# The last layer (768 to 512) as seven products over halves instead of plain blocks

## Chip, cores and metric

The kernel runs on one core of a Trainium2 chip. The metric is the time of one execution on the device in microseconds (us); before the change the median of three runs is 1456.44 us (1456.42 to 1460.39).

## What is computed

A linear attention with a norm, then an MLP with softplus, then an MLP with the maximum of three products; 4608 tokens, all in fp32.

```python
kv = einsum('bhsd,bhse->bhde', k, v)                    # 64 x 64 per head
x = q @ kv;  x = x / sqrt(mean(x*x) + 1e-06) * g_norm   # 4608 x 512
g = softplus(x @ w_in)                                  # 512 -> 2048
x = g @ w_out                                           # 2048 -> 512
h = maximum(maximum(x @ w1, x @ w2), x @ w3)            # 512 -> 768
out = h @ moe2_w_out                                    # 768 -> 512: the last layer
```

## The kernel before

The tokens are cut into five passes of 2 x 464 (the last 2 x 448). Features lie on the 128 partitions, the tokens of one half (t = 0 or 1) in a tile's columns. A pass has four stages: H (16 row blocks of w_in, softplus), X (w_out), layer 2 (w1, w2, w3 and their maximum) and the last layer. The attention of the next pass runs beside layer 2.

H, X and layer 2 multiply 2 x 2 blocks (rows by halves, inputs by halves, tokens by halves) in seven products instead of eight: `product` forms product m = 1 to 7 of a group g of two row blocks into the PSUM banks X, Y and W (`BANK`), and `sums` (L350) adds them up. Products 1, 6, 7 and 4 go into one X bank one after another; between them ACT copies the bank out, and VectorE adds Y or W to the copy. Group starts are 7 steps apart while a group spans 13 (`SLOT`), so the products of two groups alternate on TensorE. The inputs of the seven products are made by `combine` (L289): differences on VectorE and GpSimd, then each is split into hi and lo halves (an fp32r cast on ACT and a subtraction, `split`, L120). In passes 1 to 4 a product block is three fp32r matmuls (`mm3`, L130 to 134: hi x hi, hi x lo, lo x hi); in pass 0 it is one fp32 matmul on weights converted there (`to_f32`).

The weights of passes 1 to 4 come as split units of up to two product numbers from DRAM (`load_unit`, L183) into a ring of four tiles `u` (two `u3` for half units, one `ux` for a group's first). Weights that are converted late in pass 0 (`LATE`, and the last layer's) are kept there unsplit; pass 1 loads them as fp32 (`load_sums`, tile `st`, two buffers), splits them on ACT and VectorE into `u` (`split_unit`) and stores the unit for passes 2 to 4 (`make_later`, L210).

The last layer alone has plain blocks (`out_part`, L696): output block e = 0 to 3 and token half t, sums over six row blocks f in two parts (4 and 2). One loaded unit serves both t. Its input is the split maximum (`hl`, `hh`, L668 on), the lo half on GpSimd. In passes 1 to 3 the next pass's first two H groups are stretched and start `SHARED` = 12 steps early, so that they alternate with the parts of the last layer.

All work is put in as events with a time in steps (`at`); one step is about six matmuls. The framework then orders each engine's instructions by priorities and its own estimates; an engine works in that order.

Of the kernel before, what the change touches and what calls it, by code (L numbers as in the profile page):

```python
# [1 line left out]

# [14 lines left out]
P = 128  # L17
# [22 lines left out]
SHARED = 12  # L40
# [5 lines left out]
def kernel(  # L46
# [54 lines left out]
    def ge_tile(p, name, n):  # L101
        return gc_tile(name, n) if p == 0 else wide(pools["ge"], "ge", GE_BUFS, name, n)
# [62 lines left out]
    G_2 = [[16 + 3 * f + j for j in range(3)] for f in range(NF2 // 2)]  # L165
    UNITS = ((1, 5), (6, 2), (7, 4), (3,))
# [84 lines left out]

    def convert(g, i):
        if i == 0:
            sw[g] = pools["raw"].tile([P, 7, 256], F32, tag="sw", bufs=3, name="sw")
        w = sw[g]
        if i == 0:
            dst = w[:, PLACE[1]:PLACE[2] + 1:PLACE[2] - PLACE[1]]
        else:
            dst = w[:, PLACE[5]:PLACE[4] + 1:PLACE[4] - PLACE[5]]
        to_f32(raws.pop((g, i)), dst)  # L260

    def sums_of_weights(g):
        w = sw[g]
        a11, s1, s2, a12, s3, a22, s4 = (w[:, PLACE[m]] for m in (1, 5, 6, 2, 7, 4, 3))
# [14 lines left out]
    def convert_out(j, i):  # L279

        if i == 0:
            sw["o", j] = pools["raw"].tile([P, 3, 512], F32, tag="sw", bufs=3, name="swo")
        to_f32(raws.pop(("o", j, i)), sw["o", j][:, i])

# [4 lines left out]
    def combine(tile, dst, c, tiles, steps, t2_bank, on_dve=()):  # L289
# [4 lines left out]
        for s in steps:  # L294
            for m in STEPS[s]:
                hi, lo = tile("hi", n, F32R), tile("lo", n, F32R)
                src = {1: b11, 2: b21, 3: b22, 7: b12, 4: b11}.get(m)
# [3 lines left out]
                elif m == 6:  # L301
                    src = t2 = psum(t2_bank, "t2")[:, 0:n]
# [37 lines left out]
    def run_group(base, p, g, rhs, after, stretch=1):  # L340
# [6 lines left out]
        for m in ORDER:  # L347
            at(base + stretch * SLOT[m], step, m)
# [219 lines left out]
    def run_pass(pas, base):  # L568
# [5 lines left out]
        def weights_at(t, g, stretch=1):  # L574
# [35 lines left out]
        for fp in range(8):  # L610
            t = start[f"H{fp}"]
            weights_at(t, G_H[fp], stretch.get(f"H{fp}", 1))
            run_group(t, pas, G_H[fp], R,
                      sums(lambda w, src, fp=fp: h_done(fp, w, src), lambda w: (ctile(f"h{w}", N), w != 11),
                           nc.vector if pas and fp == 0 else nc.scalar),
                      stretch.get(f"H{fp}", 1))
        for n in range(4):
            gc[n] = {}
            if n == 0 or pas == 0:
                for c in range(2):  # L620
                    at(start[f"H{2 * n + c}"] + 12 * stretch.get(f"H{2 * n + c}", 1) + 0.5, combine_g, n, ALL, (c,))
# [34 lines left out]
        hh = {}  # L656
        mx = {}

        def h2_done(fp, j, w, src):
# [9 lines left out]
            if j == 2:  # L669
                src = mx.pop(key)  # L670
                at_ = 2 * fp + w // 20, w % 10 - 1
                if pas == 0:
                    hh[at_] = src
                else:
                    hi, lo = gc_tile("hh", N, F32R), gc_tile("hl", N, F32R)
                    split(nc.scalar, src, hi, lo, nc.gpsimd)
                    hh[at_] = (hi, lo)

        for k in range(9):
            fp, j = divmod(k, 3)  # L680
            t = base2 + 7 * k
            weights_at(t, G_2[fp][j])
            run_group(t, pas, G_2[fp][j], R2,
                      sums(lambda w, src, fp=fp, j=j: h2_done(fp, j, w, src),
                           lambda w, j=j: ((ge_tile(pas, f"m{w}", N), True) if j == 0
                                          else (ctile(f"m{w}", N), w == 22))))
# [179 lines left out]
```

## Time and profile before

| | before |
|---|---|
| median of 3 runs | 1456.44 us (1456.42 to 1460.39) |
| profiled execution | 1454.81 us, span 1453.0 us, mean granted clock 0.996 |
| TensorE (PE) busy | 1412.1 us, 97% |
| VectorE (DVE) / ScalarE (ACT) / GpSimd (POOL) busy | 52% / 50% / 46% |
| DMA | 315.5 MB, 217 GB/s on average |

The profile shows one execution. Its own time is larger than its span by 1.8 us, which lie around the span. "PE" is TensorE's matmuls, "PEld" its weight loads, which overlap; a matmul's duration overlaps with the next one's, so spacing is read from starts. "ACT", "DVE" and "POOL" are ScalarE, VectorE and GpSimd; "SP" issues the DMAs. In tile names u, u3, ux are weight units, st fp32 weights to be split, Xh, Xx, Xo (Y, W) the banks of H, X and layer 2, oacc the last layer's, Xy, Yy, Wy those of the last layer after the change, m the maxima, og the attention's output.

### The profile page before, as it was taken

How to read it: one execution, taken by the hardware profiler on the slowest of the kernel's cores; microseconds unless marked ns; L12 is line 12 of the kernel's file. 1: busy time of each engine (PE TensorE's matmuls, PEld its weight loads, DVE VectorE, ACT ScalarE, POOL GpSimd, SP SyncE). 2: the span in 40 equal slices, each digit the busy share in tenths (PEclk: the TensorE clock that was granted, in tenths of full speed). 3: DMA queues.
4: the chain of work that ended last, by engine and by line, in shares of the span. 5: the costliest groups of instructions: out<-in, count | busy, mean ns of one | idle time of the engine just before them, and what ended most of it. 6: DMA issues, size and time to landing. Idle time of an engine off the chain costs nothing.

```text
span 1453.0 us, 18314 instructions
## 1 busy us (share of the span) xinstructions
PE 1412.1 (97%) x6164; PEld 1126.8 (78%) x6164; DVE 761.4 (52%) x1204; ACT 719.6 (50%) x1370; POOL 671.7 (46%) x613
## 2 busy tenths in 40 slices
PE   6899999999999999999999999999999999999998
PEld 4344445554688888788888898888889888998998
DVE  4654565677144566763445557144574544447341
ACT  5566545565164437754543466254436634543321
POOL 3697778444044453452534335343463453435211
PEclk9999999999999999999999999999999999999999
DMA  7677778854366776866667776566666656676672
GB/s 279 225 253 250 272 250 315 303 176 138 129 211 210 217 242 222 266 239 200 203 209 220 247 257 193 171 209 211 217 214 207 201 181 206 211 219 208 195 219 93
DMA packets 107948, 315.51 MB, mean 217 GB/s; under 512 B 12112, under 2 KB 23632, under 8 KB 107856
## 3 DMA queue, kind: packets, MB, share of 16 engines
q1 hardware_dynamic: 107856, 314.36, 66.5%
q8 instruction: 49, 0.80, 0.3%
q14 instruction: 43, 0.35, 0.1%
HBM read 248.78 MB, written 65.54 MB: 216 GB/s over the span
## 4 chain that ended last, share of the span: by engine, by line
PE 83%; DMA 5%; DVE 4%; ACT 3%; issue 2%; POOL 2%; SPq 0%; ACTq 0%; POOLq 0%; DVEq 0%
PE Xh L132 4%; PE Xx L134 4%; PE Xx L132 4%; PE Xx L133 4%; PE Xh L134 4%; PE Xh L133 4%; PE Xo L133 3%; PE Xo L132 3%; PE Xo L134 3%; PE Xo L330 3%; PE Xh L330 3%; PE oacc L704 3%; PE oacc L133 3%; PE oacc L134 2%; PE oacc L132 2%
## 5 line engine op out<-in xcount | busy, mean ns | idle before, releaser
L122 POOL TENSOR_TENSOR lo<-e,hi 128x464 fp32r<-128x464 f32 (+1 forms) x160 | 187.4, 1202 | 216.8 <-ACT hi L116 213.3
L128 POOL TENSOR_TENSOR e<-e 128x464 f32<-128x464 f32 (+1 forms) x40 | 50.6, 1264 | 157.2 <-DVE t L128 157.2
L116 ACT COPY m<-Xo 128x464 f32<-128x464 f32 (+1 forms) x135 | 72.3, 541 | 81.3 <-PE Xo L134 71.3
L116 ACT CAST hi<-t 128x464 fp32r<-128x464 f32 (+1 forms) x96 | 52.3, 545 | 121.3 <-DVE e L128 56.3
L125 DVE TENSOR_TENSOR x<-x,Xx 128x464 f32<-128x464 f32 (+1 forms) x120 | 75.6, 632 | 61.9 <-PE Xx L134 55.2
L122 POOL TENSOR_TENSOR hl<-m,hh 128x464 fp32r<-128x464 f32 (+1 forms) x48 | 58.8, 1227 | 97.0 <-ACT hh L116 96.9
L122 POOL TENSOR_TENSOR u<-sw,u 128x512 fp32r<-128x512 f32 (+1 forms) x76 | 87.9, 1184 | 19.2 <-ACT u L116 19.0
L116 ACT CAST hi<-e 128x464 fp32r<-128x464 f32 (+1 forms) x160 | 85.7, 578 | 21.9 <-PE Yx L133 18.7
L526 POOL TENSOR_TENSOR og<-og,r 128x464 f32<-128x464 f32 (+1 forms) x32 | 41.2, 1289 | 107.5 <-DVE r L516 103.1
L152 ACT ACTIVATE e<-h 128x464 f32<-128x464 f32 (+1 forms) x80 | 47.3, 591 | 82.5 <-DVE h L125 81.9
L132 PE MATMUL Xo<-hi,u 128*128 128x464 f32 (+1 forms) x228 | 86.6, 380 | 1.2 <-ACT m L116 1.2
L134 PE MATMUL Xo<-hi,u 128*128 128x464 f32 (+1 forms) x228 | 84.8, 372 | 0.0
L133 PE MATMUL Xo<-lo,u 128*128 128x464 f32 (+1 forms) x228 | 84.8, 372 | 0.0
L116 ACT COPY h<-Xh 128x464 f32<-128x464 f32 (+1 forms) x108 | 58.7, 544 | 47.6 <-PE Xh L134 33.0
L128 POOL TENSOR_TENSOR sw<-sw 128x256 f32<-128x256 f32 x75 | 56.7, 756 | 48.5 <-DVE sw L243 34.8
L125 DVE TENSOR_TENSOR h<-h,Yh 128x464 f32<-128x464 f32 (+1 forms) x80 | 50.6, 633 | 52.7 <-ACT h L116 25.0
L125 DVE TENSOR_TENSOR Wh<-h,Wh 128x464 f32<-128x464 f32 (+1 forms) x40 | 25.7, 642 | 93.5 <-PE Wh L134 67.1
L132 PE MATMUL Xh<-hi,u 128*128 128x464 f32 (+1 forms) x194 | 72.3, 373 | 0.0
L122 DVE TENSOR_TENSOR lo<-t,hi 128x464 fp32r<-128x464 f32 (+1 forms) x96 | 60.4, 633 | 22.0 <-ACT hi L116 20.8
L134 PE MATMUL Xh<-hi,u 128*128 128x464 f32 (+1 forms) x194 | 71.8, 370 | 0.0
L133 PE MATMUL Xh<-lo,u 128*128 128x464 f32 (+1 forms) x194 | 71.8, 370 | 0.0
L132 PE MATMUL Xx<-hi,u 128*128 128x464 f32 (+1 forms) x192 | 71.2, 371 | 0.0
(223 smaller groups left out, 4096.7 us busy)
## 6 DMA issues: line engine op xcount, KB each, us to landing
u<-wd SPq DMA_DIRECT2D x198, 512.0 KB, 4.4
ux<-wd SPq DMA_DIRECT2D x96, 512.0 KB, 3.5
wd<-u SPq DMA_DIRECT2D x79, 512.0 KB, 2.8
u<-wd SPq DMA_DIRECT2D x106, 256.0 KB, 3.8
raw<-in_w_out_dram SPq DMA_DIRECT2D x22, 512.0 KB, 4.0
k<-in_kp_dram SPq DMA_DIRECT2D x32, 320.0 KB, 4.7
v<-in_vp_dram SPq DMA_DIRECT2D x32, 320.0 KB, 5.3
raw<-in_w_dram SPq DMA_DIRECT2D x18, 512.0 KB, 4.3
```

The costliest lines, as they stand in the source:

```text
L116: nc.scalar.copy(hi, src)
L122: eng_lo.tensor_tensor(out=lo, in0=src, in1=hi.bitcast(F32), op=ALU.subtract)
L125: eng.tensor_tensor(out=o, in0=a, in1=b, op=ALU.add)
L128: eng.tensor_tensor(out=o, in0=a, in1=b, op=ALU.subtract)
L132: nc.tensor.matmul(acc, wh, xh, start=first, stop=False, skip_group_check=on)
L133: nc.tensor.matmul(acc, wh, xl, start=False, stop=False, skip_group_check=on)
L134: nc.tensor.matmul(acc, wl, xh, start=False, stop=last, skip_group_check=on)
L152: tables["used"].append(nc.scalar.activation(out, src, func, **kw).ins)
L330: nc.tensor.matmul(acc, w[:, c * P:(c + 1) * P], rhs[m, c], start=first and c == 0, stop=c == 1, skip_group_check=not first)
L526: nc.gpsimd.tensor_tensor(out=og, in0=og, in1=r, op=ALU.mult)
L704: nc.tensor.matmul(acc[e, t], w[:, o * P:(o + 1) * P], hh[f, t], start=f == 0, stop=f == NF2 - 1)
```

## The change

The last layer's weights are laid out as three more groups (`G_O`, 25 to 27) of two row blocks. In pass 0 each group is converted and summed like the others (`convert`, `sums_of_weights`: four 128 x 256 sums on GpSimd) and stored block by block in the order of use (`keep_out`, `OUT_SEQ`). The maxima of each fp are combined for seven products (`combine_max`) instead of only split. The layer is then 42 blocks: output half e = 0, 1, product m, and c = 0 to 2 over three pairs of input blocks; `OPENING` products 1, 5, 2 of both e with c = 0, 1 first, then their c = 2, then `CLOSING` 6, 7, 4, 3 of e = 0, then of e = 1, each over c = 0 to 2. Units hold four blocks and serve once: eleven a pass, ten of them of full size. The results go through `sums`; `SHARED` and `stretch` are gone, so that the events of the next pass's H0 begin when those of the last layer end.

```diff
-SHARED = 12
...
+    OPENING, CLOSING = (1, 5, 2), (6, 7, 4, 3)
+    PLACE_O = {m: i for i, m in enumerate(OPENING + CLOSING)}
+    OUT_SEQ = [(e, m, c) for e in range(2) for m in OPENING for c in range(2)]
+    OUT_SEQ += [(e, m, 2) for e in range(2) for m in (1, 2)] + [(e, 5, 2) for e in range(2)]
+    OUT_SEQ += [(e, m, c) for e in range(2) for m in CLOSING for c in range(3)]
+    OUT_AT = {b: i for i, b in enumerate(OUT_SEQ)}
+    OUT_UNITS = [(4 * i, min(4, len(OUT_SEQ) - 4 * i)) for i in range(-(-len(OUT_SEQ) // 4))]
...
-        if pas > 1:
-            start["H0"], start["H1"] = base - SHARED, base + 1
-        stretch = {"H0": 1.75, "H1": 1.3} if pas > 1 else {}
...
-                src = mx.pop(key)
...
-                    hi, lo = gc_tile("hh", N, F32R), gc_tile("hl", N, F32R)
-                    split(nc.scalar, src, hi, lo, nc.gpsimd)
...
+        def combine_max(fp, steps):
+            tiles = [mx[fp, w] for w in TILES]
+            if pas == 0:
+                combine32(gc_tile, R3, fp, tiles)
+            elif fp < 2:
+                combine(gc_tile, R3, fp, tiles, steps, None)
+            else:
+                tile = ctile if steps in ((0,), (2,)) else partial(ge_tile, pas)
+                combine(tile, R3, fp, tiles, steps, None, (1, 2))
...
+            if j == 2:
...
+                    for n, s, dt in ((0, 0, slot[2] + 0.5), (1, 2, slot[4] + 0.5)):
+                        at(t + dt, combine_max, fp, (s,))
+                    at(t + slot[3] + 0.5, combine_max, fp, (1, 3, 4, 5))
...
+        def out_done(e, w, src):
+            if w == 21:
+                bank, src = src, ctile("o21", N)
+                nc.scalar.copy(src, bank)
+            r, a = 2 * (w // 20) + e, TOK[pas] + (w % 10 - 1) * N
+            nc.sync.dma_start(out=out[r * P:(r + 1) * P, a:a + N], in_=src)
...
+            if c == 2:
+                ends[e](m, {k: v[:, 0:N] for k, v in b.items()})
...
+        for i, n in OUT_UNITS if pas else ():
+            key, size, ti = ("o", i // 4), n // 2, t + 0.5 * i
             if pas == 1:
...
+                make_later(ti, key, size, None, i * P, n * P)
+            else:
+                at(ti - (6 if i == 0 else LEAD), load_unit, pas, key, size, i == 0)
+        for i, b in enumerate(seq):
+            at(t + 0.5 * i, out_block, *b)
+        return t + 0.5 * len(seq) - 0.05
```

The order on the engines moves in three places. The first is ACT in pass 1, in the last layer: casts of weight units (u from st), of the next pass's inputs (hi from og, t) and of the maxima (hh). Before:

```order
L116 CAST hi_5092<-og_4523 128x464
L116 CAST hh_5108<-m12_4748 128x464
L116 CAST hi_5096<-og_4623 128x464
L116 CAST hi_5132<-og_4103 128x464
L116 CAST hi_5136<-og_4200 128x464
L116 CAST hi_5170<-og_4737 128x464
L116 CAST hi_5174<-og_4843 128x464
L722 COPY osb_5167<-oacc_5053 128x464
L116 CAST u_5234<-st_5159 128x512
L116 CAST u3_5187<-st_5130 128x256
L722 COPY osb_5196<-oacc_5115 128x464
```

With the change (hi from t1_5174 is the third block of product 5; o11 are results; u_5219, u_5240 and u_5272 the seventh, eighth and ninth unit):

```order
L116 COPY o11_5278<-Xy_5222 128x464
L116 CAST hi_5146<-og_4349 128x464
L116 CAST u_5219<-st_5094 128x512
L116 CAST hi_5150<-og_4456 128x464
L116 CAST hi_5208<-og_4583 128x464
L116 CAST hi_5212<-og_4683 128x464
L116 CAST hi_5172<-t1_5174 128x464
L116 CAST u_5240<-st_5136 128x512
L116 CAST hi_5247<-og_4146 128x464
L116 CAST hi_5251<-og_4243 128x464
L116 CAST hi_5290<-og_4789 128x464
L116 CAST u_5272<-st_5202 128x512
```

Where two of the last layer's units stood behind the layer's own casts, the seventh now stands ahead of the hi cast of product 5, with three casts of the next pass's inputs between.

The second is TensorE in pass 2, in the last layer. Before, a part of one bank ends and the next pass's H0 (Xh) follows, then another bank:

```order
L133 MATMUL oacc_7779<-hl_7656,u3_7713 128x464
L134 MATMUL oacc_7779<-hh_7655,u3_7713 128x464
L132 MATMUL Xh_7844<-hi_7637,ux_7792 128x464
L133 MATMUL Xh_7844<-lo_7638,ux_7792 128x464
L134 MATMUL Xh_7844<-hi_7637,ux_7792 128x464
L132 MATMUL Xh_7844<-hi_7641,ux_7792 128x464
L133 MATMUL Xh_7844<-lo_7642,ux_7792 128x464
L134 MATMUL Xh_7844<-hi_7641,ux_7792 128x464
L132 MATMUL oacc_7853<-hh_6983,u_7736 128x464
```

With the change, the end of product 6 of e = 0 (Xy_7833, c = 1 and 2) and the start of product 7, on the same bank:

```order
L134 MATMUL Xy_7833<-hi_7583,u_7794 128x464
L132 MATMUL Xy_7833<-hi_7870,u_7831 128x464
L133 MATMUL Xy_7833<-lo_7871,u_7831 128x464
L134 MATMUL Xy_7833<-hi_7870,u_7831 128x464
L132 MATMUL Xy_7833<-hi_7261,u_7831 128x464
L133 MATMUL Xy_7833<-lo_7262,u_7831 128x464
```

And the end of product 7 of e = 0, four matmuls of e = 1 (Xy_7909), and the start of product 4:

```order
L134 MATMUL Xy_7833<-hi_7877,u_7831 128x464
L132 MATMUL Xy_7909<-hi_7254,u_7916 128x464
L133 MATMUL Xy_7909<-lo_7255,u_7916 128x464
L134 MATMUL Xy_7909<-hi_7254,u_7916 128x464
L132 MATMUL Xy_7909<-hi_7583,u_7916 128x464
L132 MATMUL Xy_7833<-hi_7265,u_7892 128x464
```

No part of a bank had to be copied out and used on before; now the bank Xy_7833 is, once with nothing and once with four matmuls in between.

The third is GpSimd in pass 0, in the last layer: the inputs of pass 1 (og and lo). Before:

```order
L128 TENSOR_TENSOR og_2073<-og_2229,og_2073 128x464
L128 TENSOR_TENSOR og_2150<-og_2305,og_2150 128x464
L122 TENSOR_TENSOR lo_2447<-og_1912,hi_2446 128x464
L122 TENSOR_TENSOR lo_2451<-og_2002,hi_2450 128x464
L122 TENSOR_TENSOR lo_2467<-og_2073,hi_2466 128x464
L122 TENSOR_TENSOR lo_2471<-og_2150,hi_2470 128x464
L122 TENSOR_TENSOR lo_2489<-og_1710,hi_2488 128x464
L122 TENSOR_TENSOR lo_2493<-og_1802,hi_2492 128x464
```

With the change (m12_2240 and t4_2487 are the layer's own inputs, sw_2495 the sums of the third weight group; the second of these four, line L125, is the weight of product 5):

```order
L128 TENSOR_TENSOR m12_2240<-m22_2271,m12_2240 128x464
L128 TENSOR_TENSOR t4_2487<-m21_2323,t2_2486 128x464
L122 TENSOR_TENSOR lo_2471<-og_1912,hi_2470 128x464
L122 TENSOR_TENSOR lo_2475<-og_2002,hi_2474 128x464
L122 TENSOR_TENSOR lo_2502<-og_2080,hi_2501 128x464
L122 TENSOR_TENSOR lo_2506<-og_2157,hi_2505 128x464
L122 TENSOR_TENSOR lo_2529<-og_1710,hi_2528 128x464
L128 TENSOR_TENSOR sw_2495<-sw_2495 128x256
L122 TENSOR_TENSOR lo_2533<-og_1802,hi_2532 128x464
L125 TENSOR_TENSOR sw_2495<-sw_2495 128x256
L122 TENSOR_TENSOR lo_2554<-og_2236,hi_2553 128x464
L128 TENSOR_TENSOR sw_2495<-sw_2495 128x256 x2
```

Two subtractions of the layer's inputs come ahead of the lo halves, and four sums of the third group among them.

## Rows read from the trace of the kernel before

**Rows 1.** The page, parts 1 and 2: span, engines, granted clock in 40 slices.
```profile
span 1453.0 us, 18314 instructions
...
PE 1412.1 (97%) x6164; PEld 1126.8 (78%) x6164; DVE 761.4 (52%) x1204; ACT 719.6 (50%) x1370; POOL 671.7 (46%) x613
...
PEclk9999999999999999999999999999999999999999
```
**Rows 2.** Windows: us, busy of PE, PEld, DVE, ACT, POOL, granted clock, DMA share, GB/s.
```profile
347.00:388.00 41.00, 41.00 (x106) 19.85 (x105) 14.13 (x23) 11.10 (x21) 10.30 (x9) 1.00 0.22 84
...
500.00:628.00 128.00, 123.20 (x597) 106.94 (x596) 94.12 (x142) 80.18 (x153) 59.18 (x47) 1.00 0.73 237
628.00:650.00 22.00, 20.75 (x98) 17.90 (x97) 15.54 (x27) 12.19 (x24) 15.98 (x14) 1.00 0.74 254
...
901.00:935.00 34.00, 34.00 (x163) 30.29 (x162) 12.63 (x22) 11.12 (x21) 16.27 (x14) 1.00 0.59 183
```
**Rows 3.** PE's waits: us in total, times, longest.
```profile
PE Yo L132 <- DVE m L668: 1.9, 2, 1.5
...
PE Xo L132 <- ACT m L116: 1.2, 2, 1.0
```
**Rows 4.** Timeline of PE, pass 1 (13 products) and pass 0: start, us.
```profile
448.64 0.37 PE L133 MATMUL Xh<-lo,ux 128*128 128x464 f32 x1
...
451.15 0.37 PE L133 MATMUL Xh<-lo,u 128*128 128x464 f32 x1
...
377.58 11.06 PE L704 MATMUL oacc<-m,swo 128*128 128x464 f32 x28
```
**Rows 5.** Timeline of all engines, last layer of pass 4: an eviction.
```profile
1447.80 0.36 PE L134 MATMUL oacc<-hh,u 128*128 128x448 f32 x1
...
1448.25 0.54 ACT L722 COPY osb<-oacc 128x448 f32<-128x448 f32 x1 [6.79 <-PE oacc L134]
```
**Rows 6.** Timeline of ACT, end of layer 2 of pass 1.
```profile
625.75 0.55 ACT L116 COPY m<-Xo 128x464 f32<-128x464 f32 x1 [0.26 <-POOL og L526]
629.30 0.62 ACT L116 CAST u<-st 128x512 fp32r<-128x512 f32 x1 [3.00 <-DMA st<-ws]
629.83 0.57 ACT L116 CAST hh<-m 128x464 fp32r<-128x464 f32 x1
630.30 0.54 ACT L116 COPY m<-Xo 128x464 f32<-128x464 f32 x1
```
**Rows 7.** Timeline of PE at the same place.
```profile
629.48 0.37 PE L132 MATMUL oacc<-hh,u 128*128 128x464 f32 x1
630.89 0.48 PE L132 MATMUL Xo<-hi,u 128*128 128x464 f32 x1 [1.04 <-ACT m L116]
```
**Rows 8.** Windows about the start of layer 2 in pass 4, columns as in 2.
```profile
1340.00:1342.00 2.00, 0.16 (x2) 0.10 (x1) 1.77 (x4) 2.00 (x5) 1.93 (x2) 1.00 0.67 235
1342.00:1344.00 2.00, 1.59 (x4) 1.01 (x5) 2.00 (x3) 0.29 (x1) 2.00 (x2) 0.81 0.36 120
1344.00:1346.00 2.00, 2.00 (x6) 1.39 (x6) 1.37 (x3) 1.61 (x4) 2.00 (x3) 0.50 0.00 0
1346.00:1348.00 2.00, 2.00 (x10) 1.82 (x9) 0.86 (x2) 1.61 (x4) 1.91 (x3) 0.84 0.86 250
```
**Rows 9.** DMA issues: KB each, median us to landing; all loads of tile u.
```profile
u<-wd SPq DMA_DIRECT2D x198, 512.0 KB, 4.4
...
st<-ws SPq DMA_DIRECT2D x22, 256.0 KB, 3.3
...
DMA to landing us min/median/max: 2.0/4.1/7.6
```
**Rows 10.** Groups by form, POOL: xcount, busy us, mean ns, idle before.
```profile
L122 POOL TENSOR_TENSOR lo<-og,hi 128x464 fp32r<-128x464 f32 x30 | 36.4, 1244 | 12.7 <-ACT hi L116 12.3 <-PE Yo L134 0.4
...
L128 POOL TENSOR_TENSOR sw<-sw 128x256 f32<-128x256 f32 x75 | 56.7, 756 | 48.5 <-DVE sw L243 34.8 <-PE Xo L330 7.5 <-issue 2.0
```
**Rows 11.** Timeline of POOL: its first work after the last layer of pass 0.
```profile
395.76 1.20 POOL L122 TENSOR_TENSOR lo<-e,hi 128x464 fp32r<-128x464 f32 x1 [32.06 <-ACT hi L116]
```

More of the change, by code (lines that the diff above doesn't have):

```diff
@@ L1 @@
 from contextlib import ExitStack
+from functools import partial
 import concourse.bass as bass
@@ L165 @@
     G_2 = [[16 + 3 * f + j for j in range(3)] for f in range(NF2 // 2)]
+    G_O = [25 + j for j in range(3)]
     UNITS = ((1, 5), (6, 2), (7, 4), (3,))
@@ L219, in raw_of @@
             return [w_out[2 * (g - 8) + i] for i in range(2)]
+        if g in G_O:
+            return [w2_out[2 * (g - G_O[0]) + i] for i in range(2)]
         f, j = divmod(g - 16, 3)
@@ L254, in convert @@
             sw[g] = pools["raw"].tile([P, 7, 256], F32, tag="sw", bufs=3, name="sw")
[L255 to L259, printed above, removed]
+        a, b = (place(g)[m] for m in ((5, 4) if i else (1, 2)))
+        dst = sw[g][:, a:b + 1:b - a]
         to_f32(raws.pop((g, i)), dst)
@@ L263, in sums_of_weights @@
         w = sw[g]
[L264 removed]
+        a11, s1, s2, a12, s3, a22, s4 = (w[:, place(g)[m]] for m in (1, 5, 6, 2, 7, 4, 3))
         sub(nc.gpsimd, s3, a11, s1)
@@ new lines, in run_pass, with out_block @@
+        banks, ends = {}, {}
+        def out_done(e, w, src):
[4 more added lines that the diff above has]
+            nc.sync.dma_start(out=out[r * P:(r + 1) * P, a:a + N], in_=src)
+        for e in range(2):
+            banks[e] = {}
+            ends[e] = sums(lambda w, src, e=e: out_done(e, w, src), lambda w: (ctile(f"o{w}", N), True))
+        def out_block(e, m, c):
+            tag, b = BANK[m], banks[e]
+            first = m in OPENING
+            if first and c == 0:
+                b[tag] = psum("at" if tag == "W" else tag, f"{tag}y")
+            acc = b[tag][:, 0:N]
+            if pas == 0:
+                g, h = divmod(3 * e + c, 2)
+                w = sw[G_O[g]][:, PLACE_O[m], h * P:(h + 1) * P]
+                nc.tensor.matmul(acc, w, R3[m, c], start=first and c == 0, stop=c == 2, skip_group_check=not first)
+            else:
+                i, k = divmod(OUT_AT[e, m, c], 4)
+                u = units[pas, ("o", i)]
+                if u.shape[1] == 2:
+                    wh, wl = (u[:, r, k * P:(k + 1) * P] for r in range(2))
+                else:
+                    wh, wl = (u[:, 0, r + k * P:r + (k + 1) * P] for r in (0, 256))
+                xh, xl = R3[m, c]
+                mm3(acc, wh, wl, xh, xl, first and c == 0, c == 2, not first)
+            if c == 2:
+                ends[e](m, {k: v[:, 0:N] for k, v in b.items()})
```

124 lines of the change are left out of this document (45 added, 79 removed).

## The prediction

> **What bounds the kernel now.** I read the page first [rows 1]: TensorE is busy 97% of a span of 1453.0 us, at full granted clock nearly throughout, and no other engine is above 52%. The windows by stage say the same of the stretches that the change touches [rows 2]: while the last layer runs, in pass 0 (347 to 388 us) and at the end of pass 2 (901 to 935 us), PE is busy all the time; only pass 1's (628 to 650 us) has a hole of 1.25 us. The list of PE's waits has two rows that matter later [rows 3]. So the time is the number of products times their spacing plus PE's holes. A product taken away is gained in full, and a hole that opens is lost in full; what VectorE, ScalarE (ACT) and GpSimd (POOL) do besides costs nothing unless a product stands behind it.
>
> The spacing is not the duration in the groups (372 ns), which overlaps with the next product. Twelve steps of a 464-wide product take 451.15 - 448.64 = 2.51 us, so 0.209 us each; a 448-wide one is put at 0.209 x 448/464 = 0.202. An fp32 product of pass 0 leaves two records, 28 of which took 11.06 us with the last one's 0.55 in it: 10.51/27 = 0.389 each, 0.78 a product [rows 4].
>
> **What is removed.** Seven products over halves replace eight: 2 x 7 x 3 = 42 blocks where 4 x 2 x 6 = 48 stood. Pass 0: 6 x 0.78 = 4.7 us. Passes 1 to 3: 18 matmuls x 0.209 = 3.76 us each, 11.3 together. Pass 4: 18 x 0.202 = 3.6 us. Sum 19.6 us. The hole of pass 1 goes too, in half: it came from an ACT copy behind a weight split that waited 3.00 us for its load [rows 6, 7], and the new order has that kind of split at the same place; I take 0.6 of 1.25.
>
> **What is added, first: hand-overs of a bank.** In the closing stage products 6, 7 and 4 of one half add into the same X bank, and ACT must copy the bank between them. The price from rows: last matmul's start to the copy's start 1448.25 - 1447.80 = 0.45, the copy 0.54 [rows 5], the copy's end to PE's next start 630.89 - 630.84 = 0.05 [rows 6, 7]; less the spacing, 0.83 us. Four other products in between (4 x 0.21 = 0.84) cover it. By the order of PE, in passes 2 and 3 three of four hand-overs have four products between them (those of e = 0 or of the next pass's H0, so the overlap is not wholly gone) and one has none; in pass 4, without a next pass, three have none. 5 x 0.83 = 4.2 us; between 0, if other products' lateness hides them, and all 12 of these passes, 10.0. I take the count by the order. In pass 0 an fp32 product of 0.78 stands in between each time: nothing.
>
> **Second: ACT's order in pass 1.** Here each weight unit is loaded as fp32 and split by ACT and VectorE into one of four buffers. Before, a two-row unit served two token halves, 24 products; now 12, so the ring of four turns twice as fast. In the new ACT order the split of the seventh unit (u_5219) takes the third's buffer, whose last readers are the twelve-block opening's end, directly ahead of the third block of product 5. Behind it in ACT stand three casts of the next pass's inputs and only then that block's hi cast. ACT starts casts 0.47 to 0.53 us apart [rows 6]: 0.45 + 4 x 0.5 + 0.55 + 0.05 - 0.21 = 2.8 us of waiting where nothing is left to do, and 0.2 for the lo on VectorE. The ninth unit waits for the fifth, which that block ends; two casts, then product 6's hi: 0.45 + 2 x 0.5 + 0.55 + 0.05 - 0.21 = 1.8, less four products (0.8): 1.0. The copy of the first hand-over comes late by 0.45 (two products between, casts ahead). The tenth unit waits for the sixth, and the second hand-over's copy is behind it: 0.45 + 0.5 + 0.54 + 0.05 - 0.21 = 1.3. Sum 5.75 us. Bounds: 1.25 (the hole that is there now) and 10 (each of the five units that reuse a ring buffer holding up a cast by 2.0). I take the walk. The loads are just in time: 3.3 us median [rows 9] against about 3.5 from buffer to use.
>
> **The clock.** Where PE starved ahead of layer 2 in pass 4 (0.16 us busy in 1340 to 1342), the granted clock fell to 0.50, that is from 2.4 to 1.2 GHz, and cost at most 2 x (0.19 + 0.50 + 0.16) = 1.7 us [rows 8]. The wait of 2.8 us in pass 1 should bring that once; the slower products let the casts catch up, so I charge half, 0.9. The Trainium skill (TensorE: Matmul & The Clock Gate, "A second HAM failure mode: psum-queue depth-cycling") has a rule that speaks against this change: small idles of TensorE between groups that take turns on PSUM banks make the clock swing between its levels, again and again. The trace does not bear that out for single holes: 500 to 628 us has one of 1.5 and a granted clock of 1.00 [rows 2, 3]. By the rule five hand-overs would add 8.5 us; by the rows nothing.
>
> **Third: POOL in pass 0.** Before, the last layer's weights went from the load to PE; now each pair of row blocks takes four sums of 756 ns on POOL [rows 10], 12 in all. Eight fall in layer 2, hidden. Those of the third group stand in POOL's order among the lo halves of the next pass's inputs, at about 1.2 us each. Before, POOL was through with all of these 32.06 us ahead of 395.76, at 363.7 [rows 11]. Now three of them come later (-3.6), two subtractions of the layer's own inputs (+2.4) and two sums (+1.5) earlier, and one lo stands between the sums (counted in the three, so +1.2): the second sum is there at 365.2. The product that needs it is the 23rd of the layer's order, 22 x 0.78 = 17.2 us after 347, at 364.2. I charge 1.0 us, between 0 (POOL got its casts earlier) and 4.3 (the other two lo halves, and two sums that did not find room in layer 2).
>
> **Rest.** Nine more casts a pass on ACT, 17 more VectorE operations and four more on POOL in layer 2 lie beside products: 0.5 us in all, between 0 and 2. The third block of product 7 gets its lo from POOL behind eight others: 0.2 in passes 2 and 3 each. SP now issues eleven unit loads instead of eight in passes 2 to 4; the eviction at the very end is one VectorE operation and a store as before.
>
> **Sum:** -19.6 - 0.6 + 4.2 + 5.75 + 0.9 + 1.0 + 0.5 + 0.4 = about -7.4 us. The profiled execution took 1454.81 us; the median of the three runs is 1456.44, 1.6 above. I put the difference on the median: **1449.0 us**. A measurement of this kernel can tell about 0.3% (4.4 us) from no change.
>
> **Rivals.** (A) The forecast: somewhere between -4.4 and -10 us, chance 0.47.
> (B) ACT and POOL get there in time: the waits of pass 0 and pass 1 (1.0, and 5.75 + 0.9 - 0.65 for what stays of the old hole) fall away, -14.4 us, **1442 us**. For it: in the last layer as it stands PE is kept waiting 1.25 us in pass 1 and not at all in passes 0 and 2 [rows 2]. Against: the ring of four. Chance 0.17.
> (C) The clock falls at each of the five uncovered hand-overs, 1.7 us each: -7.4 + 8.5, **1457.5 us**, no change to be told. Against it the row of 1.00 above; the rule named above is for it. Chance 0.08.
> (D) The same waits at their upper bounds, 4.3 in pass 0 and 10 in pass 1: 3.3 + 4.25 more, **1456.6 us**, no change. Chance 0.14.
> (E) Slower: the ring of four weight buffers in passes 2 to 4. A unit's buffer comes free when its 12 products end, and the unit that takes it is due after three others, 3 x 12 x 0.209 = 7.5 us later. If a load then takes L us, each turn waits L - 7.5, two turns a pass, three passes: 6 x (L - 7.5). Slower by 0.3% needs 11.8 us more than the sum, so L = 9.5; at L = 10 it is 15 - 7.4 = +7.6 us, **1464 us**. For it: the layer asks 512 KB every 2.5 us, 209 GB/s, with the stores on top, where 183 GB/s are moved now [rows 2]. Against it: the loads land in 4.4 us median and 7.6 at most [rows 9]. Chance 0.14.
> That the overlap is not dropped in fact, because the order still puts H0's first products into the gaps, is part of A.
>
> **Numbers.** Faster is A and B, 0.64; within 0.3% C and D, 0.22; slower E, 0.14. The range 1439 to 1457.5 us takes in A, B and D with the bounds of the hand-overs (4 us either way), leaving out E, half of C and a little below: under 0.2.
>
> **What would show it.** Right: 42 x 3 products at 0.21 in the last layer of passes 1 to 4; PE waits for ACT hi casts in pass 1's last layer of 3 to 6 us; a hole of 0.8 before product 7 of the first half in passes 2 and 3, three in pass 4; a dip of the granted clock in pass 1 alone. Wrong: PE waiting for unit loads there (E), dips in each pass (C), or no waits for ACT in pass 1 (B). If layer 2 ahead of it grew by more than 2 us a pass, the cost that I put at 0.5 would be the mistake.

## The result, and the profile after

The changed kernel is slower: 1468.95 us median of 11 runs (1464.99 to 1474.53) against 1459.87 of 11 runs of the kernel before (1456.42 to 1465.04), a ratio of 1.0062 with a 95% interval of 1.0045 to 1.0078. That is 6.6 to 11.4 us more, where I had forecast 7 less. A second set of runs gave 1.0063 (1.0045 to 1.0081).

The profiled execution of the changed kernel took 1469.18 us. The one of the kernel before, on which the sum was made, took 1454.81, below all its 11 runs. So differences of profiles are made below against the profile of a kernel that e4 runs.

The page of the changed kernel, against [rows 1]:

```profile
span 1467.4 us, 18433 instructions
...
PE 1403.7 (96%) x6080; PEld 1109.7 (76%) x6080; DVE 819.6 (56%) x1291; ACT 746.1 (51%) x1429; POOL 706.9 (48%) x647
```

PE has 84 records fewer, the 6 x 2 of pass 0 and 18 in each of the other four passes, so the products did go. But its busy time fell by only 8.4 us while the span grew by 14.4: it stands idle 22.8 us longer. The windows of the last layer say where (us, busy time of PE, PEld, DVE, ACT and POOL, granted clock, DMA share, GB/s, as in [rows 2]):

```profile
352.00:396.00 44.00, 39.79 (x101) 19.21 (x100) 19.03 (x31) 13.94 (x26) 19.96 (x20) 0.96 0.31 103
372.00:382.00 10.00, 7.59 (x16) 3.66 (x17) 0.25 (x1) 0.55 (x1) 6.02 (x7) 0.83 0.38 126
637.00:677.00 40.00, 32.72 (x143) 25.47 (x142) 25.34 (x38) 18.45 (x36) 16.92 (x13) 1.00 0.80 264
...
650.00:660.00 10.00, 7.54 (x31) 5.02 (x30) 9.16 (x13) 8.20 (x17) 8.97 (x7) 1.00 0.72 234
...
918.00:952.00 34.00, 31.89 (x150) 27.29 (x149) 16.10 (x28) 13.61 (x27) 15.40 (x13) 1.00 0.70 222
```

In pass 0 (352 to 396 us) PE is idle for 4.2 us where it was busy throughout [rows 2], and the granted clock falls to 0.83 in the ten microseconds from 372. In pass 1 (637 to 677) it is idle for 7.3 us, and from 650 to 660 VectorE and GpSimd are nearly full; in pass 2 it is idle for 2.1. PE's waits in the same kernel (total, times, longest) answer to [rows 3]:

```profile
PE Xy L132 <- ACT o L116: 4.8, 7, 1.2
PE Xy L133 <- POOL lo L122: 4.3, 3, 2.0
PE Yy L740 <- POOL sw L125: 3.7, 1, 3.7
...
PE Yo L132 <- DVE m L683: 3.5, 2, 3.0
PE Xh L132 <- DMA ux<-wd: 3.0, 3, 2.0
...
PE Yy L132 <- ACT hi L116: 1.9, 1, 1.9
```

The tiles Xy, Yy and Wy are the last layer's banks. None of their waits is for a weight load; they are for ACT, for GpSimd and for VectorE. The two longest single waits (3.7 and 2.0 us) are for GpSimd; of the two rows that they stand in I had priced one at 1.0 and the other at 0.4.

### The profile page after: what moved, and what is told of

Its sections match the earlier page's. It is cut to its first block, busy times and chain, and to the rows that moved or that the text cites. A ratio compares the mean times of both kernels' runs of the same rounds, so it can differ in the third digit from the quotient of the medians.

```text
span 1467.4 us, 18433 instructions
## 1 busy us (share of the span) xinstructions
PE 1403.7 (96%) x6080; PEld 1109.7 (76%) x6080; DVE 819.6 (56%) x1291; ACT 746.1 (51%) x1429; POOL 706.9 (48%) x647
## 4 chain that ended last, share of the span: by engine, by line
PE 76%; DMA 8%; DVE 6%; ACT 4%; issue 2%; POOL 2%; SPq 1%; ACTq 0%; DVEq 0%; POOLq 0%
PE Xx L134 4%; PE Xx L132 4%; PE Xx L133 4%; PE Xh L132 4%; PE Xh L134 3%; PE Xh L133 3%; PE Xo L132 3%; PE Xo L133 3%; PE Xo L134 3%; PE Xh L350 3%; PE Xo L350 2%; PE Yh L133 2%; PE Yh L132 2%; PE Yh L134 2%; PE Yx L132 2%
## 5 line engine op out<-in xcount | busy, mean ns | idle before, releaser
L116 ACT CAST hi<-t 128x464 fp32r<-128x464 f32 (+1 forms) x120 | 65.1, 544 | 141.8 <-DVE t L128 56.1
L125 DVE TENSOR_TENSOR x<-x,Xx 128x464 f32<-128x464 f32 (+1 forms) x120 | 75.5, 631 | 61.9 <-PE Xx L134 55.3
L116 ACT CAST hi<-e 128x464 fp32r<-128x464 f32 (+1 forms) x160 | 85.1, 579 | 21.9 <-PE Yx L133 18.7
L122 POOL TENSOR_TENSOR lo<-m,hi 128x464 fp32r<-128x464 f32 (+1 forms) x52 | 63.2, 1234 | 65.0 <-ACT hi L116 64.9
L122 DVE TENSOR_TENSOR lo<-t,hi 128x464 fp32r<-128x464 f32 (+1 forms) x120 | 75.5, 634 | 29.7 <-ACT hi L116 26.5
L125 DVE TENSOR_TENSOR Wh<-h,Wh 128x464 f32<-128x464 f32 (+1 forms) x40 | 25.7, 642 | 115.8 <-PE Wh L134 88.7
L128 POOL TENSOR_TENSOR sw<-sw 128x256 f32<-128x256 f32 x84 | 63.3, 753 | 50.1 <-DVE sw L246 34.9
L125 DVE TENSOR_TENSOR h<-h,Yh 128x464 f32<-128x464 f32 (+1 forms) x80 | 50.5, 631 | 43.9 <-PE Yh L134 17.5
L241 DVE SCALAR_TENSOR_TENSOR cv<-cv,raw 128x512 int32<-128x512 int32 x56 | 39.0, 697 | 58.2 <-ACT raw L240 36.6
```

The lines of the kernel that those rows point to most:

```text
L116: nc.scalar.copy(hi, src)
L122: eng_lo.tensor_tensor(out=lo, in0=src, in1=hi.bitcast(F32), op=ALU.subtract)
L125: eng.tensor_tensor(out=o, in0=a, in1=b, op=ALU.add)
L128: eng.tensor_tensor(out=o, in0=a, in1=b, op=ALU.subtract)
L241: nc.vector.scalar_tensor_tensor(out=u, in0=u, scalar=3, in1=lo32, op0=ALU.logical_shift_left, op1=ALU.bitwise_or)
```

## The experiments

Theory W, formed from these rows: the loss is waits in the last layer, each behind an engine's queue in which the layer's own work stands after the next pass's inputs (tiles og, and their hi and lo). The rivals are that the dropped overlap costs the time (O), and that a wait taken away only moves (M).

**e1: one queue, one kind of operation.** The lo halves of the layer's third block go to VectorE.

```diff
-                combine(tile, R3, fp, tiles, steps, None, (1, 2))
+                combine(tile, R3, fp, tiles, steps, None, (1, 2, 7, 4, 3))
```

> Edit: in the changed kernel the lo halves of products 7, 4 and 3 of the last layer's third block go to VectorE in passes 1 to 4; nothing else moves. Theory W (the 16 us that I missed are waits of TensorE in and around the last layer, each behind a queue that this layer shares with the next pass's inputs): the three waits of TensorE for a lo of GpSimd at product 7 (1.97, 1.42 and 0.96 us in passes 1, 2 and 3) go, and pass 4 stays as it is: 4.3 us less than the changed kernel, a ratio to before of about 1.0032 where the changed kernel has 1.0062. Rival M (the waits only move: the products behind are held by ACT's bank copies and casts just as long): the waits for GpSimd go and others in the same layer grow by as much; ratio 1.006.

Measured: 1.0027 (1.0010 to 1.0044). The wait for a lo of GpSimd at product 7 is gone from the list in all three passes; in pass 1 a wait of VectorE's lo half grew from 1.05 to 2.77 us. As W says, with some of M in pass 1. What had happened is in the timeline of GpSimd in pass 1 of the changed kernel (start, us, line, operation, tiles):

```profile
656.46 6.72 POOL L122 TENSOR_TENSOR lo<-og,hi 128x464 fp32r<-128x464 f32 x5
663.15 3.62 POOL L122 TENSOR_TENSOR lo<-m,hi 128x464 fp32r<-128x464 f32 x3
```

and in that of PE at the same place, with the idle time ahead of a row and what ended it in brackets:

```profile
662.19 0.37 PE L132 MATMUL Xy<-hi,u 128*128 128x464 f32 x1
664.54 0.47 PE L133 MATMUL Xy<-lo,u 128*128 128x464 f32 x1 [1.97 <-POOL lo L122]
664.86 0.37 PE L134 MATMUL Xy<-hi,u 128*128 128x464 f32 x1
```

Five lo halves of the next pass's inputs (og) take 6.72 us; the layer's own (m) come after them. The PE rows also show that a wait costs more than its idle time: from 662.19 to 664.86 two matmuls start in 2.67 us where 0.42 is the spacing, 2.25 lost for an idle of 1.97.

**e2: all these queues at once.** The next pass's inputs 6 units later.

```diff
-                at(base3 - 2 + SLOT[ms[-1]] + 0.5, combine_x, pas + 1, (s,))
+                at(base3 + 4 + SLOT[ms[-1]] + 0.5, combine_x, pas + 1, (s,))
```

> Edit: in the changed kernel the next pass's inputs are made 6 units later (the time argument of combine_x alone), so that on ACT, VectorE and GpSimd the last layer's own casts, copies and sums come ahead of theirs. Theory W: the waits of TensorE in the last layer fall away: 3.7 us in pass 0 with 1.7 us of slow clock behind it, 4.3 us for GpSimd's lo at product 7, and 3 of the 5 us for ACT in pass 1, together 12.7 us; what is given back at the start of the next pass, whose eight lo halves on GpSimd (1.2 us each) now end later, is at most 2 us a pass where a first product waits. Between 1456 and 1464 us, ratio 0.998 to 1.002. Rival M: the next pass's first group starts as much later as the layer ends earlier, ratio 1.005 to 1.008. Rival O (what costs is the dropped overlap, not the shared queues): no gain, and the first group waits longer, ratio above 1.008.

Measured: 0.9983 (0.9965 to 1.0000). From 1.0062 to here are 0.8%, 11.5 us, by one number. M and O fall. PE no longer waits for GpSimd in the last layer, but a new wait, for loads, stands on the list of e2's waits (and one of 1.2 us in pass 1 for VectorE's half of a weight split):

```profile
PE Xy L132 <- DMA u<-wd: 3.9, 2, 2.1
PE Xy L132 <- ACT o L116: 3.4, 4, 1.5
```

**e3: pass 0 alone.** The third weight pair's sums on VectorE.

```diff
-        sub(nc.gpsimd, s3, a11, s1)
...
+        eng = nc.vector if g == G_O[2] else nc.gpsimd
+        sub(eng, s3, a11, s1)
...
```

> Edit: in the changed kernel the four sums of the third weight pair of the last layer of pass 0 go from GpSimd, where they stand among the lo halves of the next pass's inputs, to VectorE. Theory W: the wait of 3.66 us for a GpSimd sum at 374 us goes, and with it the stretch at a granted clock of 0.83 behind it (1.7 us): 5.4 us less than the changed kernel, about 1463.6 us, ratio 1.0025. Rival M: the raw weights come too late from the load for any engine, and TensorE waits for VectorE instead, 2 us or more: ratio 1.005 to 1.006.

Measured: 1.0032 (1.0014 to 1.0049). In the changed kernel the timeline of GpSimd in pass 0 reads:

```profile
365.00 1.17 POOL L128 TENSOR_TENSOR t<-m,t 128x464 f32<-128x464 f32 x1 [0.58 <-DVE t L128]
366.12 5.76 POOL L122 TENSOR_TENSOR lo<-og,hi 128x464 fp32r<-128x464 f32 x5
371.84 0.72 POOL L128 TENSOR_TENSOR sw<-sw 128x256 f32<-128x256 f32 x1
372.52 1.16 POOL L122 TENSOR_TENSOR lo<-og,hi 128x464 fp32r<-128x464 f32 x1
373.64 0.72 POOL L125 TENSOR_TENSOR sw<-sw 128x256 f32<-128x256 f32 x1
```

and PE's next product after it:

```profile
374.41 1.91 PE L740 MATMUL Yy<-t,sw 128*128 128x464 f32 x2 [3.66 <-POOL sw L125]
```

With the sums on VectorE, e3's windows there show PE nearly full at a full clock:

```profile
362.00:372.00 10.00, 9.40 (x25) 4.27 (x24) 9.36 (x13) 6.67 (x13) 8.52 (x8) 1.00 0.12 43
372.00:382.00 10.00, 10.00 (x28) 4.75 (x26) 2.77 (x5) 1.09 (x2) 3.66 (x3) 1.00 0.49 168
```

So the wait of 3.66 us brought the clock's fall with it (10 us at 0.83, by estimate 10 x 0.17 = 1.7 us), and both went together.

**e4: the other half of the change.** The kernel before, without its overlap.

```diff
-        if pas > 1:
-            start["H0"], start["H1"] = base - SHARED, base + 1
-        stretch = {"H0": 1.75, "H1": 1.3} if pas > 1 else {}
+        stretch = {}
...
-                t += (2, 1)[part] * (1 if i < 4 or pas in (0, NPASS - 1) else 1.6)
+                t += (2, 1)[part]
-        if 0 < pas < NPASS - 1:
-            t -= 7.2
```

> Edit: the kernel before, with the eight plain products of the last layer, but its overlap with the next pass's first groups dropped (no SHARED, no stretch, no earlier base). Theory W: the overlap is worth the wait for the second group's first weight load, which has one buffer (1.96, 0.57 and 0.51 us in the changed kernel against 0.33, 0.26 and 0.62 before): 1 to 3 us slower than before, ratio 1.001 to 1.002. Rival O (the dropped overlap is the cause of the loss): 9 us or more slower than before, ratio 1.006 or more. If it is the same or faster the overlap is worth nothing and the whole loss belongs to the seven products.

Measured: 0.9996 (0.9983 to 1.0008). With the plain blocks the overlap was worth nothing that can be measured, less than the 1 to 3 us that W had expected, and O falls: the loss belongs to the seven products. What the overlap would give beside them was not tried. Its only wait for ux is 0.2 us, less than in the kernel before.

**e5: the step of the prediction that blamed the ring of four.**

```diff
-        u = units[1, key] = unit_tile(size, 1)
+        u = units[1, key] = unit_tile(size, 1, key == ("o", 6))
```

> Edit: in the changed kernel the last layer's seventh weight unit of pass 1 gets a buffer of its own (the one called ux, which pass 1 does not use there) in place of its turn in the ring of four. Theory P (the step of my prediction: the split of that unit stands on ACT for its buffer, and product 5's last hi cast stands behind it): TensorE's wait of 1.87 us for that cast and part of the 1.20 us for the copy after it go, 2 to 3 us less than the changed kernel. Rival V (VectorE, 9.2 us busy of 10 from 650 to 660 us, makes that cast's source late; the ring has little to do with it): the wait for the hi cast stays within 0.4 us of 1.87, and the time within 1 us. The first group of pass 2 loads into the same buffer later than it did and may wait up to 1 us longer in either theory; the rows of TensorE's waits tell the two apart, the time of the whole run hardly.

Measured: 1.0074 (1.0054 to 1.0094), no gain. The wait for the hi cast is 2.20 us against 1.87. The seventh unit's split moved to its own buffer, and no time came of it: P falls. V holds for the wait; the time is 1.7 us up where V had allowed 1, which the two intervals do not tell apart. The timeline of VectorE in the changed kernel shows why:

```profile
650.89 0.62 DVE L683 TENSOR_TENSOR m<-m,Yo 128x464 f32<-128x464 f32 x1
651.50 1.28 DVE L122 TENSOR_TENSOR u<-st,u 128x512 fp32r<-128x512 f32 x1
652.70 1.64 DVE L128 TENSOR_TENSOR t<-m,m 128x464 f32<-128x464 f32 x1
```

and ACT's cast of that t:

```profile
654.37 0.55 ACT L116 CAST hi<-t 128x464 fp32r<-128x464 f32 x1 [1.46 <-DVE t L128]
```

The maximum that product 5 needs is there at 651.5. Then a weight split (u, 1.28) stands ahead of the subtraction t, which itself takes 1.64 us in place of 0.64 (the last section has more on this). ACT waits 1.46 us for VectorE, not for a buffer.

**e6: the wait that e2 uncovered.** On top of e2, unit 6 in the buffer of unit 0.

```diff
-                at(ti - (6 if i == 0 else LEAD), load_unit, pas, key, size, i == 0)
+                at(ti - (6 if i == 0 else LEAD), load_unit, pas, key, size, i in (0, 24))
```

> Edit: on top of the next pass's inputs 6 units later, unit 6 of the last layer is loaded into the buffer of unit 0 (ux) in passes 2 to 4, so that it does not wait for unit 2's turn in the ring of four. Theory L (behind the queues that the later inputs freed, the ring of four weight buffers is next: the waits of 1.84 and 2.05 us for a unit's load in passes 2 and 3 are its turns): both waits go, 3.9 us less than with the later inputs alone, ratio to before about 0.9956. Rival T (the load is late because the transfers or SyncE's queue are full, not for want of a buffer): waits of 1 to 2 us for loads stay, at this unit or the next, ratio 0.998.

Measured: 0.9952 (0.9936 to 0.9969); both waits for loads are gone. So they were turns of the ring, as L says. But the order of TensorE in e2 shows why the ring was short there. Pass 2, the end of product 6 of e = 0 (Xy_7797) and the first closing product of e = 1 (Xy_7865), with the numbers of the weight buffers in the order in which they were loaded (7786, 7795, 7848, 7872):

```
L134 MATMUL Xy_7797<-hi_7826,u_7795 128x464
L132 MATMUL Xy_7865<-hi_7254,u_7872 128x464
L133 MATMUL Xy_7865<-lo_7255,u_7872 128x464
L132 MATMUL Xy_7797<-hi_7261,u_7795 128x464
```

The row of the filler's first matmul in e2's timeline of PE, and the one ahead of it:

```profile
921.97 0.37 PE L134 MATMUL Xy<-hi,u 128*128 128x464 f32 x1
924.17 0.45 PE L132 MATMUL Xy<-hi,u 128*128 128x464 f32 x1 [1.84 <-DMA u<-wd]
```

The two matmuls that were put into the hand-over to fill it use a unit (7872) that is loaded after one not yet used (7848). The filler itself waits 1.84 us, to save a hand-over of 0.7 us.

**e7: the halves in turn.** On top of e2, the closing products alternate between e = 0 and e = 1, so a hand-over has three of the other half's blocks (nine matmuls, 1.9 us) in between, and the units are used in the order of loading.

```diff
-    OUT_SEQ += [(e, m, c) for e in range(2) for m in CLOSING for c in range(3)]
+    OUT_SEQ += [(e, m, c) for m in CLOSING for e in range(2) for c in range(3)]
```

> Edit: on top of the next pass's inputs 6 units later, the closing products of the two halves take turns (product 6 of e = 0, of e = 1, product 7 of e = 0, of e = 1, and so on), in every pass but the first. Theory H (a bank hand-over costs TensorE its 0.6 to 0.9 us only where fewer than four other products stand in between): the three waits of 0.68, 0.68 and 0.62 us in pass 4 go, with the restart of 0.1 each, 2.2 us in all, and the 1.46 us of pass 1: 2 to 3.7 us less than with the later inputs alone, ratio to before 0.9958 to 0.997; the waits for unit loads stay. Rival B (with both halves open the six banks are held longer and the next pass's first products wait for one): the waits for ACT's copies go, and as much comes back at the start of passes 2 to 4; ratio 0.998.

Measured: 0.9903 (0.9886 to 0.9921), 1444.33 us against 1458.45. It is faster than both kernels, and by more than H gave (0.9958 to 0.997): the hand-overs of pass 4 went (no wait of PE is left there), but the waits for loads went too, where I had expected them to stay. In pass 1 H fails: its wait for a copy did not go, 0.64 and 2.24 us stand there in place of 1.46. The rows account for about 7 us of the step from 0.9983 (the waits for loads and the hand-overs, with their restarts); the rest, some 4 us, is not placed, and e8 and e11, with the same order, read 0.9923. The next pass's first product no longer starts inside this layer (it starts at 663.6 us, 0.2 after the layer's last; in the changed kernel at 672.2, 4.5 ahead of it). The windows of its last layer in passes 2 and 3:

```profile
902.00:932.00 30.00, 30.00 (x145) 26.73 (x144) 18.56 (x30) 13.78 (x28) 16.70 (x14) 1.00 0.78 249
1165.00:1195.00 30.00, 30.00 (x144) 26.71 (x143) 18.40 (x30) 13.84 (x28) 16.37 (x14) 1.00 0.76 245
```

**e8: all three.** e7's diff, with e6's:

```diff
+                at(ti - (6 if i == 0 else LEAD), load_unit, pas, key, size, i in (0, 24))
```

> Edit: the next pass's inputs 6 units later, unit 6 in the buffer ux, and the halves in turn. If the three costs are separate, as theories W, L and H say, their gains add: about 6.5 us less than with the later inputs alone, ratio to before 0.993 to 0.995, some 1449 us on the chip of the last call. If they hide one another, as a rival, it is no better than the better of the two alone, 0.9956 or more.

Measured: 0.9923 (0.9908 to 0.9939); its interval overlaps e7's. It lies below both expected ranges, as e7 alone does, and the extra buffer adds nothing that can be measured once the units are used in order: L and H were not separate costs.

**e9: the halves in turn on the changed kernel itself**, without e2's edit.

```diff
+    OUT_SEQ += [(e, m, c) for m in CLOSING for e in range(2) for c in range(3)]
```

> Edit: in the changed kernel only the closing products of the two halves take turns; the next pass's inputs stay where they are. The same edit on top of the later inputs gave 11 us (0.9983 to 0.9903 of before). Theory S (the two edits mend different waits: this one the three hand-overs of pass 4, 2.2 us, the ones of 0.69 in passes 2 and 3, and the load of H1's first unit, 2 to 3 us in all, because H0's first products are no longer drawn into the gaps; the waits for GpSimd and VectorE behind the next inputs stay): 5 to 7 us less than the changed kernel, ratio to before 1.001 to 1.003. Rival J (each needs the other, since the products that fill the gaps are late behind the next inputs anyhow): 0 to 3 us, ratio 1.004 to 1.006.

Measured: 1.0021 (1.0006 to 1.0035). As S says. The wait for GpSimd's sum (3.64 us) and those behind VectorE stay; the three hand-overs of pass 4 are gone. One thing S did not expect: the waits for GpSimd's lo at product 7 fell from 4.3 us in three to 1.9 in two.

**e10: the changed kernel again.**

> No edit: the changed kernel once more, on the chip of its neighbours and with a second profile, to see which waits are its own and which belong to one execution. The theory of the shared queues expects the same rows: 3.7 us for GpSimd's sum in pass 0, 4 to 4.4 us for GpSimd's lo at product 7, 1.9 us for the hi cast in pass 1, three hand-overs of 0.6 to 0.7 in pass 4; the wait for ux at the start of pass 2 (1.96) and the 3.01 us in layer 2 of pass 1 may differ by 1 us. Ratio to before 1.0045 to 1.0078, as measured.

Measured: 1.0063 (1.0045 to 1.0081). The list of PE's waits in its profile:

```profile
PE Xy L132 <- ACT o L116: 4.8, 7, 1.2
PE Xy L133 <- POOL lo L122: 4.3, 3, 2.0
PE Yy L740 <- POOL sw L125: 3.6, 1, 3.6
...
PE Yy L132 <- ACT hi L116: 1.9, 1, 1.9
...
PE Yo L132 <- DVE m L683: 1.3, 2, 0.9
...
PE Xh L132 <- DMA ux<-wd: 1.0, 3, 0.5
```

The first four are the kernel's own, to a tenth. The other two differ from one execution to the next: the longest wait of layer 2 in pass 1, 3.0 us in the first profile, is 0.9 here and 1.8 to 2.9 in the other kernels with the seven products (1.5 in both without them); the one for ux, 2.0 us, is at most 0.5 here. The granted clock in pass 1 differs too. It was 1.00 from 637 to 677 us in the first profile; here it falls behind the waits of 1.98 and 1.20 us (at 663.0 and 664.9), as it does in e7 behind that of 2.24 (0.83 from 654 to 664 us):

```profile
660.00:670.00 10.00, 6.82 (x24) 5.31 (x24) 3.04 (x3) 2.46 (x5) 5.25 (x5) 0.83 0.59 228
```

**e11: 10 units later in place of 6**, on e7.

```diff
-                at(base3 + 4 + SLOT[ms[-1]] + 0.5, combine_x, pas + 1, (s,))
+                at(base3 + 8 + SLOT[ms[-1]] + 0.5, combine_x, pas + 1, (s,))
```

> Edit: halves in turn and the next pass's inputs 10 units later in place of 6. What is left in the last layer with 6 units is pass 1: 0.64 and 2.24 us for ACT's copies behind casts of the next inputs, which wait for VectorE. If that is the queue once more, part of the 2.9 us goes: 1 to 2.5 us less than with 6 units, ratio to before 0.9885 to 0.9895. Rival: the inputs become too late for the next pass's first group, and TensorE waits there for GpSimd's lo instead: ratio 0.991 to 0.994.

Measured: 0.9923 (0.9903 to 0.9943); its interval overlaps e7's. The two waits of pass 1 are still there (0.77 and 2.15 us; 0.64 and 2.24 in e7), and no wait for a lo has come: neither side is borne out. But the edit did not do what it was meant to do there. In e7's timeline of ACT, the copy that PE waits for stands behind casts of the next pass's inputs (hi from t, which VectorE makes from og), and the first of them waits for VectorE:

```profile
650.45 0.55 ACT L116 CAST hi<-t 128x464 fp32r<-128x464 f32 x1 [2.45 <-DVE og L128]
650.89 0.62 ACT L116 CAST u<-st 128x512 fp32r<-128x512 f32 x1
651.41 0.55 ACT L116 CAST hi<-t 128x464 fp32r<-128x464 f32 x1
651.85 0.56 ACT L116 COPY o<-Xy 128x464 f32<-128x464 f32 x1
```

In e11's, with the later time, the order is the same:

```profile
650.77 0.55 ACT L116 CAST hi<-t 128x464 fp32r<-128x464 f32 x1 [2.36 <-DVE og L128]
651.21 0.62 ACT L116 CAST u<-st 128x512 fp32r<-128x512 f32 x1
651.73 0.55 ACT L116 CAST hi<-t 128x464 fp32r<-128x464 f32 x1
652.17 0.56 ACT L116 COPY o<-Xy 128x464 f32<-128x464 f32 x1
```

So by the trace it is the same queue once more, with a weight split of 1.70 us (at 648.16 in e7) ahead of the subtraction og on VectorE. VectorE is nearly full ahead of these waits in e7; what moving these casts behind the copy would give was not tried:

```profile
640.00:650.00 10.00, 9.36 (x44) 7.74 (x42) 9.38 (x13) 5.43 (x11) 5.46 (x4) 1.00 0.82 274
```

## Why the prediction was wrong

The forecast of 1449.0 us is 20.0 below the measured 1468.95. Of these, 3.4 lie in the kernel before, which measured 1459.87 where I had 1456.44; the other 16.5 are the change, +9.1 where I had -7.4. The steps that failed are two waits of TensorE for GpSimd: for a sum in pass 0, put at 1.0 us, and for the lo halves at product 7, put at 0.4 (both below).

Where the time went, stage by stage, from the start of the first product of the X groups in one pass to the same in the next (the last to the end of the span). In e4, without the change and without the overlap, these starts are 96.1, 426.1, 699.5, 970.3 and 1235.2 us, the end 1456.0; in e10, the changed kernel, 96.9, 429.2, 709.7, 980.8, 1245.4 and 1463.9; in e7 95.8, 422.0, 696.9, 965.2, 1227.4 and 1444.3. "Added" is the pass less the same pass in e4, plus what the products take off. Two profiles of the changed kernel differ by up to 3 us in a pass (pass 1: 280.5 in e10, 711.4 - 427.8 = 283.6 in the first), so only the large entries mean something.

| pass | products off | added, forecast | added, e10 | added, e7 |
|---|---|---|---|---|
| 0 | 4.7 | 1.0 | 7.0 | 0.9 |
| 1 | 3.8 | 6.1 | 10.9 | 5.3 |
| 2 | 3.8 | 1.0 | 4.1 | 1.3 |
| 3 | 3.8 | 1.0 | 3.5 | 1.1 |
| 4 | 3.6 | 2.5 | 1.3 | -0.3 |
| all | 19.6 | 11.6, and 0.5 anywhere | 26.8 | 8.3 |

**Right: what is removed.** Counting products at their spacing holds inside the layer. In e7, whose last layer has no hole in passes 2 to 4, it is 3.9, 3.8 and 3.7 us shorter there than in e4 (29.18, 29.23 and 28.26 us against 33.05, 33.00 and 31.96), where I had 3.8, 3.8 and 3.6. The whole passes 2 and 3 are 2.5 and 2.7 us shorter: most of the rest is given back between the layer's end and the next X group (33.9 and 33.0 us against 33.0 and 32.1). There TensorE waits for a load of ux (0.28 and 0.35 us), and the matmuls around it start up to 0.76 us apart in place of 0.21; e4 has no such wait there. Of the old hole of pass 1, 1.25 us, 0.40 is left where I had 0.65.

**Right: the hand-overs.** One of 0.69 us of idle in passes 2 and 3 each, and 0.68, 0.68 and 0.62 in pass 4, at the places that the order gave: 3.4 us, and with 0.28 of restart each, as in the rows of e1, 4.8 against 4.2 forecast. They do not make the clock swing: it is granted in full from 918 to 952 us, and in the last layers of passes 3 and 4 as well (1.00 from 1184 to 1219 and from 1432 to 1464 us), so rival C falls. The Trainium skill (TensorE: Matmul & The Clock Gate, "A second HAM failure mode: psum-queue depth-cycling") has such small idles make the clock swing; these rows, with one to three of them in a layer, do not bear that out.

**Wrong: "POOL in pass 0": 1.0.** It measured 3.63 to 3.66 us of wait, and 1.7 of slow clock behind it, which I had looked for in pass 1 alone. The step that failed is when GpSimd's queue begins: I had worked back from the old finish of the lo halves, 363.7. But the order has them behind the layer's own last subtraction, which waits for VectorE (365.00), so they begin at 366.12, and five of the eight stand ahead of the first sum. From the layer's first product, at 352.5, the second sum is there after 374.36 - 352.5 = 21.9 us; I had put it at 365.2 - 347 = 18.2. The upper bound for the wait, 4.3, held; I had no row that spoke for a value near the lower end.

**Wrong: "the third block of product 7 gets its lo from POOL behind eight others: 0.2".** With the other term of GpSimd this is the larger part of the error. The waits are 1.97, 1.42 and 0.96 us in passes 1, 2 and 3 (1.98, 1.37 and 0.96 in e10), 4.3 in all where I had 0.4. I had seen the order, and had even counted the eight halves, but left pass 1 out and did not walk the queue with 1.2 us a step, as I did for ACT. e1 takes these waits away and the ratio falls from 1.0062 to 1.0027, some 5.1 us; e3 does it for the sum in pass 0, and the ratio falls to 1.0032, some 4.4 us. That is 9.5 us for two terms that I had put at 1.4.

**Right in size, wrong in cause: "ACT's order in pass 1", 5.75.** The waits in e10 that belong to this term are 1.03 (VectorE's lo), 1.86 and 0.55 (hi casts) and 1.20 (a copy), 4.6 us of idle and about 1 of restarts. But the ring of four buffers does not make the largest; e5 gave the unit a buffer of its own and the wait stayed. By the timeline in e5 it is VectorE's queue, which I had charged 0.2 there, an engine 52% busy over the span before. From 650 to 660 us it is 92% busy (the window above). With the next pass's inputs out of the way the wait is gone (e2); that VectorE alone makes it was not tried.

**Small: the clock in pass 1 and layer 2.** The dip in pass 1 that I charged at 0.9 is not there in the first profile and is there in e10, where it costs about twice that by the same estimate as in e3. Layer 2 ahead of the layer, from its first product to the layer's first, takes 95.3, 94.6 and 89.6 us in passes 1 to 3 of e4 and 95.5, 94.8 and 89.7 in e10, so its 0.5 was not the mistake. In the first profile passes 1 and 2 have 98.4 and 96.6, more than in e10 of the same kernel; the wait of 3.0 us is in the first of these.

**The rivals.** E, the slower one that I had thought of, did not happen: no product of the last layer waits for a unit's load in the changed kernel. The ring came into play only once the waits ahead of it were gone (e2), and through fillers used out of turn. D was nearer in kind, waits at their upper bounds in pass 0 and pass 1, but it left GpSimd in passes 1 to 3 out. What I lacked was a rival in which the next pass's inputs come ahead of the layer's own work on every engine; e2 shows that this one cause carries the change from slower to not slower, and e7 that the products removed are worth their price.

## What to carry to other kernels

An engine that is half busy over the span can be full in the ten microseconds that matter, and its queue is in order: walk it, step by step, for each operation that a product waits for. When a change puts new work on the path of a stage, look at what stands ahead of it on each engine that is due only later, and move that first; here it was one number. Work that fills a gap should draw on buffers in the order in which they are loaded; here the filler, out of that order, waited longer than the gap (1.84 us for 0.7). And a later time given to an operation is no later place in the queue: look at the order that came of it, as e11 shows.

## What the runs showed of the hardware

A subtraction on VectorE with both inputs in SBUF takes longer while GpSimd works beside it. The rows under e5 have the subtraction t from m and m in the changed kernel at 1.64 us (652.70). GpSimd's timeline there has lo halves over it, the first row; in e7 the same subtraction meets an idle GpSimd, the second row:

```profile
651.03 4.33 POOL L122 TENSOR_TENSOR lo<-og,hi 128x464 fp32r<-128x464 f32 x3 [5.06 <-ACT hi L116]
```

```profile
637.87 0.64 DVE L128 TENSOR_TENSOR t<-m,m 128x464 f32<-128x464 f32 x1
```

In every profile of the seven products this subtraction takes 0.62 to 0.65 us where no GpSimd instruction runs during it, and 0.98 to 1.65 where one does, for all of it or for half. The maximum (m from m and Yo), with one input in PSUM, takes 0.61 to 0.64 us either way in both profiles of the changed kernel. In the groups by form of e10 (count, busy us, mean ns) it shows as a longer mean of the subtraction, which mixes both cases:

```profile
L128 DVE TENSOR_TENSOR t<-m,m 128x464 f32<-128x464 f32 x12 | 9.9, 826 | 0.2
...
L683 DVE TENSOR_TENSOR m<-m,Yo 128x464 f32<-128x464 f32 x24 | 15.1, 630 | 0.3
```

The Trainium skill says of this (GPSIMD Engine Reference, "1. Specifications") that GpSimd shares its way into SBUF with VectorE and that instructions with two SBUF inputs contend. The rows agree: 0.98 to 1.65 us against 0.64. It matters here because the layer's own subtractions have two SBUF inputs and run while GpSimd makes the lo halves; that this alone decides any wait was not tried.
